# Five attention-weight transposes by DMA, with the tokens dealt otherwise to the logits' column groups, in a new order

## The chip, the cores and the metric

The kernel runs on one core of a Trainium2 chip. A core has a matrix engine (TensorE, PE in the profile, whose weight loads are listed as PEld), a vector engine (VectorE, DVE), a scalar engine (ScalarE, ACT), GpSimd (POOL) and SyncE (SP), which here issues nearly all DMAs. Each engine works through its own list of instructions in order, and they meet at semaphores. The metric is the device time of one execution in microseconds (us). Before the change it is 241.6 us, the median of 3 runs between 240.67 and 242.48.

## The reference

One transformer block over 2048 tokens of 512 features, in bfloat16, with adaptive layer norm. A conditioning vector gives six vectors of 512: shift, scale and gate for the attention half, and the same for the feed-forward half.

```python
mod = (_silu(c) @ w_mod).reshape(c.shape[0], 6, 1, -1)        # sa, ca, ga, sb, cb, gb
h = _layernorm(x, axis=-1) * (1 + ca) + sa
x = x + ga * _A_ref(h, A_wqkv, A_wo)
h = _layernorm(x, axis=-1) * (1 + cb) + sb
x = x + gb * _B_ref(h, B_w1, B_w3, B_w2)
```

`_A_ref` is local attention: 32 heads of 16 features; each token looks at itself and the 7 tokens 2, 4, ... 14 places back, positions before the start are masked, softmax over those 8, then the output projection `wo`. `_B_ref` is a gated feed-forward of width 1792: `silu(h @ w1) * (h @ w3) @ w2`.

## The kernel before, in words

The 2048 tokens are 16 tiles of 128, with tokens on the partitions (`x_sb`). Layer norm 1, its transposition (`ln_T`) and the projections q, k, v run on groups of 2, 2, 4, 4 and 4 tiles (`LN1`). q and k stay on the chip with features on the partitions; v goes to a scratch tensor in DRAM (`v_scratch_dram`) and comes back shifted.

Attention runs on pairs of tiles (`BLOCKS`: seven blocks, the last of two pairs).

- `logits`: for one tile, VectorE multiplies q with eight shifted views of k into `pq` (L742, 128 x 4096 elements). TensorE sums 16 features per head with an indicator matrix `E_sb` (L752): 16 matmuls of 32 output rows, in four column groups of the array that work side by side. Column group q gives 32 rows (the heads) of the logits for 32 tokens; a row holds 8 shifts by 32 tokens. Tile 0 starts with one more matmul (L749) that adds the mask `before`.
- `shift`, `exps`, `softmax` (L764, L769, L782, L794 to L797): maximum, subtraction, exponential, sum, reciprocal, product, on the PSUM bank of the pair; the weights `attn` are written to SBUF with the eight shifts of one token side by side.
- The weights are then turned, so that (token, shift) lies on the partitions and (token group, head) along the row: four TensorE transposes per pair (`turn`, L807) into a PSUM bank `ps_at`, and one ScalarE copy of 128 x 512 (L811) into `al`.
- `values`: four DMAs per tile (L820) gather v in the same arrangement into `vsh`; two buffers of their own and one, `vshx`, that lies where `wqkv` was. VectorE multiplies them with `al` (L827, 128 x 4096), TensorE sums over the shifts with `ind2` (L855, 32-column matmuls again), ScalarE copies (L861), a DMA transpose on SyncE's queue turns the result (`sb_ot<-sb_ac`), TensorE applies `wo` (L867), and VectorE adds it to `x_sb` with the row sum (L871).

Layer norm 2 takes that row sum: GpSimd gives the mean (L586), ScalarE the sum of squares (L590), GpSimd 1/sigma and the bias (L596, L597, L599), ScalarE the normalized tile (L601). Tiles are transposed on TensorE (L636) or by DMA (`sb_h<-sb_xn`, for groups 2 to 5) and modulated on ScalarE (L621 or L644). The feed-forward runs on groups of 2, 2, 4, 4, 2 and 2 tiles (`FFN`), 14 slices of 128 hidden features each: TensorE `w1` (L883), ScalarE Silu (L889), TensorE `w3` (L883 again), VectorE product (L892); then `w2` (L921, the last two tiles L909) and VectorE's residual addition (L931), and the store. At the start 24 matmuls on ones (L518) keep TensorE at work until the first data is there.

Nothing chooses the order of the work at run time. `_build` lists 1118 operations, each with its engine; `ORDER` is one written list of their numbers, from which every engine takes its own in that order, and `SLOTS` gives each pooled value its buffer or PSUM bank (8 banks). `synchronize` derives the waits. An operation waits for its producers and for the earlier users of its buffer; whatever stands behind it on its engine waits too. The `cost` and `dma` numbers in the calls are those of the planner that wrote the lists and have no effect in the kernel. All DMAs but one are issued by SyncE (`Program.dma`, L124).

## Time and profile before

| | before |
|---|---|
| median of 3 runs | 241.6 us (240.67 to 242.48) |
| the profiled execution | 241.33 us |
| its span | 239.6 us |
| TensorE busy | 231.9 us (97%) |
| VectorE busy | 179.2 us (75%) |
| ScalarE busy | 138.8 us (58%) |
| GpSimd busy | 30.0 us (13%) |
| L807 transposes | x32, 219 ns each, in 8 groups of four |
| L811 copies | x8, 598 ns each |
| DMA transposes | 20 of `sb_h<-sb_xn`, 16 of `sb_ot<-sb_ac` |
| moved by DMA | 38.85 MB |

The span is the time from the first to the last instruction in one profiled execution; the time of that execution is slightly longer. Busy times are unions of the instructions' records; matmuls overlap, so for TensorE the distance between starts says more than a record's length. In the lists, L12 is line 12 of the kernel, `x4` the number of instructions, and a bracket gives the idle time before an instruction and what ended it. SPq is SyncE issuing a DMA; the time from there to the landing is listed apart.

### The profile page before, as it was taken

The numbers are of one execution on the slowest core, as the hardware profiler recorded it, in microseconds if no ns is written. First come the engines' busy times: TensorE is split into PE (matmuls) and PEld (weight loads), VectorE is DVE, ScalarE is ACT, GpSimd is POOL, SyncE is SP. The second block draws the span as 40 slices with busy tenths as digits, with TensorE's granted clock in tenths as the row PEclk, the third lists the DMA queues.
The fourth block names the chain that finished last, engine by engine and source line by source line (L and its number), as shares of the span: only waits on it lengthen the run. The fifth ranks groups of instructions, "written<-read, shape, count | busy, mean of one in ns | idle before, by whom it ended". The sixth has DMA issues, their size and how long they took to land.

```text
span 239.6 us, 4572 instructions
## 1 busy us (share of the span) xinstructions
PE 231.9 (97%) x1806; PEld 135.9 (57%) x1806; DVE 179.2 (75%) x279; ACT 138.8 (58%) x267; POOL 30.0 (13%) x66
## 2 busy tenths in 40 slices
PE   7899999999999999999999999988999999999995
PEld 4676554545688684664444444433374484566774
DVE  5689999999999999999999989381555125234243
ACT  2289577899978737958735792636466043322210
POOL 4434000013002000420005220032020000000000
PEclk9999999999999999999999999999999999999999
DMA  6999999999999995998953995341300700010102
GB/s 210 373 336 309 138 244 299 214 270 310 335 291 255 250 204 168 248 191 240 228 153 90 198 228 58 96 122 36 77 22 12 100 0 0 3 43 2 47 22 66
DMA packets 46317, 38.85 MB, mean 162 GB/s; under 512 B 21704, under 2 KB 37080, under 8 KB 46296
## 3 DMA queue, kind: packets, MB, share of 16 engines
q1 hardware_dynamic: 46288, 38.56, 67.7%
q8 instruction: 14, 0.23, 0.4%
q14 instruction: 7, 0.06, 0.1%
q10 hardware_dynamic: 8, 0.00, 0.0%
HBM read 29.62 MB, written 4.21 MB: 141 GB/s over the span
## 4 chain that ended last, share of the span: by engine, by line
PE 79%; DMA 6%; DVE 5%; SPq 4%; ACT 2%; POOL 2%; issue 1%; DVEq 0%
PE pall L883 36%; PE pall L921 16%; PE pall L691 7%; PE pall L867 6%; DMA sb_x<-in_A_x_dram 5%; SPq L124 4%; PE pall L711 4%; PE pall L752 3%; PE pall L855 3%; PE pall L909 3%; DVE sb_pq L742 2%; DMA sb_ot<-sb_ac 1%; DVE sb_vsh L827 1%; POOL sb_nm L586 1%; DVE sb_st L555 1%
## 5 line engine op out<-in xcount | busy, mean ns | idle before, releaser
L883 PE MATMUL pall<-sb_h,sb_w 128*128 128x256 bf16 (+1 forms) x672 | 102.9, 308 | 1.7 <-ACT sb_sg L889 1.7
L883 PEld LDWEIGHTS pall<-sb_h,sb_w 128*128 128x128 bf16 x672 | 64.8, 98 | 38.1 <-ACT sb_sg L889 2.1
L892 DVE TENSOR_TENSOR sb_hh<-sb_sg,pall 128x256 bf16<-128x256 bf16 (+1 forms) x84 | 40.0, 506 | 37.8 <-PE pall L883 32.6
L889 ACT ACTIVATE sb_sg<-pall 128x256 bf16<-128x256 f32 (+1 forms) x84 | 35.7, 453 | 50.9 <-PE pall L883 49.0
L921 PE MATMUL pall<-sb_w,sb_hh 128*128 128x512 bf16 x196 | 45.1, 379 | 0.0
L742 DVE TENSOR_TENSOR sb_pq<-sb_q,sb_kT 128x4096 bf16<-128x4096 bf16 x16 | 36.4, 2283 | 0.0
L691 PE MATMUL pall<-sb_h,sb_wqkv 128*128 128x512 bf16 (+1 forms) x160 | 31.1, 336 | 0.4 <-DVE sb_st L555 0.4
L921 PEld LDWEIGHTS pall<-sb_w,sb_hh 128*128 128x128 bf16 x196 | 19.1, 98 | 21.2 <-issue 0.4
L827 DVE TENSOR_TENSOR sb_vsh<-sb_vsh,sb_al 128x4096 bf16<-128x4096 bf16 x12 | 27.3, 2285 | 0.0
L621 ACT ACTIVATE sb_h<-sb_h,sb_modc 128x512 bf16<-128x512 bf16 (+1 forms) x24 | 16.5, 742 | 9.5 <-DMA sb_h<-sb_xn 9.5
L691 PEld LDWEIGHTS pall<-sb_h,sb_wqkv 128*128 128x128 bf16 x160 | 14.6, 97 | 12.1 <-DVE sb_st L555 0.6
L931 DVE TENSOR_TENSOR sb_o<-pall,sb_x 128x512 bf16<-128x512 f32 (+1 forms) x18 | 11.1, 625 | 10.0 <-PE pall L921 6.2
L586 POOL TENSOR_SCALAR sb_nm<-sb_sx 128x2 f32<-128x2 f32 x8 | 3.7, 464 | 108.4 <-DVE sb_x L871 108.3
L867 PE MATMUL pall<-sb_wo,sb_ot 128*128 128x512 bf16 x64 | 15.8, 379 | 0.5 <-DMA sb_ot<-sb_ac 0.5
L711 PE MATMUL pall<-sb_wqkv,sb_h 128*128 128x512 bf16 x64 | 16.0, 379 | 0.0
L871 DVE SCALAR_TENSOR_TENSOR sb_x<-pall,sb_x 128x512 bf16<-128x512 f32 x16 | 10.9, 687 | 4.6 <-PE pall L867 4.2
L644 ACT ACTIVATE sb_h<-pall,sb_modc 128x256 bf16<-128x256 bf16 (+1 forms) x18 | 9.9, 611 | 7.5 <-DVE sb_modc L509 6.5
L590 ACT ACTIVATE sb_xn<-sb_x,sb_nm 128x512 bf16<-128x512 bf16 x16 | 11.4, 716 | 4.8 <-POOL sb_nm L586 4.8
L861 ACT ACTIVATE sb_ac<-pall 128x512 bf16<-128x512 f32 x16 | 9.4, 597 | 7.0 <-PE pall L855 6.8
L601 ACT ACTIVATE sb_xn<-sb_x,sb_nb,sb_rs 128x512 bf16<-128x512 bf16 x16 | 12.2, 804 | 1.5 <-POOL sb_nb L599 1.4
L555 DVE BATCH_NORM_STATS2 sb_st<-sb_x 128x6 f32<-128x512 bf16 x16 | 10.5, 680 | 1.4 <-DMA sb_x<-in_A_x_dram 1.4
L701 ACT ACTIVATE sb_kT<-pall 128x512 bf16<-128x512 f32 x16 | 9.6, 606 | 2.8 <-PE pall L691 2.7
(87 smaller groups left out, 206.7 us busy)
## 6 DMA issues: line engine op xcount, KB each, us to landing
sb_vsh<-v_scratch_dram SPq DMA_DIRECT2D x48, 256.0 KB, 5.4
sb_vshx<-v_scratch_dram SPq DMA_DIRECT2D x16, 256.0 KB, 5.1
sb_w<-in_B_w_dram SPq DMA_DIRECT2D x6, 512.0 KB, 7.2
sb_w<-in_B_w_dram SPq DMA_DIRECT2D x6, 384.0 KB, 4.1
v_scratch_dram<-sb_v SPq DMA_DIRECT2D x16, 128.0 KB, 6.0
out_dram<-sb_o SPq DMA_DIRECT2D x14, 128.0 KB, 1.8
sb_wqkv<-in_A_wqkv_dram SPq DMA_DIRECT2D x6, 256.0 KB, 6.5
sb_x<-in_A_x_dram SPq DMA_DIRECT2D x4, 256.0 KB, 6.5
```

What stands on the lines that cost most here:

```text
L555: o = p.op("dve", lambda e, T=T: e.bn_stats(st[:, T, :], x_sb[:, T, :]), 595, ("st", T), r=[vx[T]], w=[vs])
L601: p.op("act", lambda e, vn=vn, T=T: e.activation(vn.at[:], x_sb[:, T, :], ACT.Identity, bias=nb[:, T, :], scale=rs[:, NT + T, :]), c_act(5 ...
L621: return e.activation(vh.at[:, ft, 0:n * P], vh.at[:, ft, 0:n * P], ACT.Identity, bias=modc[:, 8 * which + ft:8 * which + ft + 1], scale=m ...
L691: ins = e.matmul(bank(vp)[:, j * n:(j + 1) * n], wqkv[:, t, col:col + P], vh.at[:, t, 0:n], start=(t == ORDER[0] and j == 0), stop=(t == O ...
L711: ins = e.matmul(bank(vp), vh.at[:, t, tt * P:(tt + 1) * P], wqkv[:, t, 2 * D:3 * D], start=(t == ORDER[0]), stop=(t == ORDER[-1]))
L742: return e.tensor_tensor(vp.at[:], in0, in1, ALU.mult)
L827: return e.tensor_tensor(v_w, v_w, a_w, ALU.mult)
L867: ins = e.matmul(bank(vy), vt.at[:, ft, :], wo[:, ft, :], start=(ft == 0), stop=(ft == KT - 1))
L883: ins = e.matmul(bank(vp)[:, 0:n], wt[:, t, fi * P:(fi + 1) * P], vh.at[:, t, 0:n], start=(t == 0), stop=(t == KT - 1))
L889: p.op("act", lambda e: e.activation(vt.at[:, 0:n], bank(vgp)[:, 0:n], ACT.Silu), c_act(n), k, r=[vgp], w=[vt], table="silu")
L892: p.op("dve", lambda e: e.tensor_tensor(vh_.at[:, 0:n], vt.at[:, 0:n], bank(vup)[:, 0:n], ALU.mult), c_dve(n), k, r=[vt, vup], w=[vh_])
L921: ins = e.matmul(bank(vz), vhh[fi].at[:, tt * P:(tt + 1) * P], w2[:, fi, :], start=(fi == 0), stop=(fi == NF - 1))
```

## The change

Before, column group q held the 32 tokens 32q to 32q + 31 of its tile, even ones first and odd ones behind. Now a column group holds one parity of two blocks of 32 tokens: group q takes the tokens 64a + 32 (q // 2) + q % 2 + 2b, for a in 0, 1 and b in 0 to 15. Each run of 16 tokens by 8 shifts of `attn` is then a plain block of 128 columns, and block after block the transposition gives `al` in the arrangement that L827 reads. That makes it one transposition of 128 x 512 in four square blocks, which a DMA can do.

- The mask for tile 0 has to reach two column groups, so L749 becomes two matmuls and the pattern of `before` changes.
- For the pairs that begin with tiles 0, 2 and 4 (`AT_PE`) TensorE and ScalarE do the turn as before. For the pairs 6, 8, 10, 12 and 14 the four transposes, the PSUM bank and the copy are replaced by one DMA transpose, issued by SyncE like all the others.
- `ORDER` and `SLOTS` are written anew, for 1113 operations and without five `ps_at` banks. The order differs on every engine. Two differences that the text below names: on SyncE the last load of x (tiles 12 to 15) comes ahead of the load of `wm_g[0]`, and on VectorE the residual additions of tiles 12 and 13, followed by one feed-forward product, come between the softmax of pair 14 and L827 of tiles 14 and 15.

```diff
     def dma(self, out, in_, key, packets, r=(), w=(), part=(), after=(), eng="sp", cost=450, group=None, transpose=False,
-            store=False, again=False, lat=None):
+            store=False, again=False, lat=None, hold=()):
...
+AT_PE = (0, 2, 4)
...
-    atb = [sb([P, 2, 32, W], bf, f"attn{i}") for i in range(NSM)]
-    alb = [sb([P, 2, 8, H], bf, f"al{i}") for i in range(3)]
+    atb = [sb([P, 2 * 32 * W], bf, f"attn{i}") for i in range(NSM)]
+    alb = [sb([P, 4, P], bf, f"al{i}") for i in range(3)]
...
-                                           pattern=[[-DIL, W], [1, 2], [2, 16]], channel_multiplier=0), 400, k, w=[vbefore])
+                                           pattern=[[-DIL, W], [64, 2], [2, 16]], channel_multiplier=0), 400, k, w=[vbefore])
...
                 if T == 0:
-                    e.matmul(PALL[0:32, c0:c0 + W * 32], ones[:, 0:32], before[:], start=True, stop=False, tile_position=(0, 0))
+                    for q in range(2):
+                        e.matmul(PALL[32 * q:32 * q + 32, c0:c0 + W * 32], ones[:, 0:32], before[:], start=True, stop=False, tile_position=(0, 32 * q))
                 for ft in range(KT):
                     for q in range(4):
-                        ins = e.matmul(PALL[32 * q:32 * q + 32, c0:c0 + W * 32], E_sb[:, ft, :], bass.AP(vp.at, ft * P + 32 * q, [[W * KT * P, P], [KT * P, W], [1, 2], [2, 16]]),
-                                       start=(ft == 0 and (T > 0 or q > 0)), stop=(ft == KT - 1), tile_position=(0, 32 * q))
+                        ins = e.matmul(PALL[32 * q:32 * q + 32, c0:c0 + W * 32], E_sb[:, ft, :], bass.AP(vp.at, ft * P + 32 * (q // 2) + q % 2, [[W * KT * P, P], [KT * P, W], [64, 2], [2, 16]]),
+                                       start=(ft == 0 and (T > 0 or q > 1)), stop=(ft == KT - 1), tile_position=(0, 32 * q))
...
-        vt, val = Val("ps_at", psum), Val("al", alpool)
+        val = Val("al", alpool)
+        if Ts[0] not in AT_PE:
+            p.dma(lambda: val.at[:], lambda: ve.at[0][:], ("at", Ts[0]), (128, 1024), r=[va], w=[val], hold=[ve], cost=1270, transpose=True)
+            return val
+        vt = Val("ps_at", psum)

         def turn(e):
             b = bank(vt).bitcast(bf)
-            for i in range(n):
-                at = b[:, i * 256:(i + 1) * 256].rearrange("p (q y h) -> p q y h", q=4, y=2)
-                for y in range(2):
-                    ins = e.transpose(at[:, :, y, :], bass.AP(ve.at[0], i * W * 32 + y * 16 * W, [[2 * W * 32, P], [1, P]]), ident[:])
+            for g in range(2 * n):
+                ins = e.transpose(b[:, g * P:(g + 1) * P], ve.at[0][:, g * P:(g + 1) * P], ident[:])
             return ins
...
 ORDER = [
...
 SLOTS = [
...
```

## The prediction

> **What bounds the kernel now.** I read the page first, then the busy times by stretch, the chain that ended last, and the timeline around the chain's only long gap.

> ```profile
> span 239.6 us, 4572 instructions
> PE 231.9 (97%) x1806; PEld 135.9 (57%) x1806; DVE 179.2 (75%) x279; ACT 138.8 (58%) x267; POOL 30.0 (13%) x66
> ...
> PE   7899999999999999999999999988999999999995
> ...
> DVE  5689999999999999999999989381555125234243
> ```

> TensorE is busy from end to end, VectorE nearly so until 150 us. The stretches (PE, PEld, DVE, ACT and POOL busy, clock, DMA share, GB/s) say it more sharply:

> ```profile
> 30.00:40.00 10.00, 10.00 (x79) 5.07 (x78) 9.94 (x12) 7.60 (x14) 0.55 (x1) 1.00 1.07 249
> ...
> 120.00:130.00 10.00, 10.00 (x87) 4.65 (x86) 10.00 (x11) 5.49 (x12) 2.07 (x2) 1.00 0.45 114
> ...
> 150.00:160.00 10.00, 10.00 (x57) 4.60 (x50) 5.61 (x10) 4.29 (x7) 2.08 (x1) 1.00 0.47 131
> 160.00:170.00 10.00, 8.10 (x48) 3.10 (x47) 4.00 (x5) 6.48 (x13) 1.55 (x4) 1.00 0.20 41
> ```

> The reader sees two engines full at once between 20 and 140 us, and one hole in TensorE at 160 to 170 us. The granted clock is 1.00 throughout, so TensorE's own steps can be added up. From one group's start to the next a feed-forward half (four matmuls, L883) takes 0.863 us at 512 columns and 0.437 at 256, seven matmuls of L921 1.51, four of L867, L711 or L691 0.863, a reduction (L752, L855) 0.44. Along the old order these steps make 231.4 us, from the first warm-up matmul at 1.24 us to the last; the trace ends them at 237.08. So 4.4 us are lost to waits: 0.9 before 58 us, 0.3 near 92, 3.05 between 155 and 174, 0.15 in small pieces. Behind the last matmul come 2.5 us of addition and store. The profiled execution took 241.33 us, 1.73 more than its span and 0.27 less than the median of the runs, 241.6. My sum is made against 241.33.

> **The change, part by part: the five transposes.** The chain shows what four transposes cost TensorE, and what a change between full-array and 32-column matmuls costs:

> ```profile
> 35.85 0.22 PE pall L807 x4
> ...
> 126.17 0.55 PE pall L855 x8
> 126.71 0.88 PE pall L752 x32
> 127.59 0.44 PE pall L855 x8
> 128.03 5.29 PE pall L883 x24
> ```

> Four transposes are one step of 0.22 us; five pairs give up 5 x 0.223 = 1.1 us, all of it on the full engine. Eight matmuls of L855 take 0.44 us behind other 32-column work and 0.55 behind L883; 24 matmuls of L883 take 5.29 behind L855 where 6 x 0.863 is 5.18. So each change of mode costs about 0.1 us. The old order of TensorE's work has 28 changes, the new one 32 (the reductions of tile pairs stand more often alone): 4 x 0.095 = +0.4 us. Tile 0's causal mask takes two small matmuls in place of one; they lie in different column groups and run together as the four groups of L752 do, under 0.1 us. Dealing the tokens otherwise keeps 16 matmuls of 256 columns per tile; only the middle step of the read pattern changes (64 tokens apart in place of 1), while the inner step stays 2 elements. Its price is not in the trace. Below, a cheaper read has nothing to give, since 16 x 256 / 4 columns already go in 0.44 us; above, four groups that no longer ran together would cost four times 0.44 on each of 16 tiles, +21 us. The inner step is the same, so I take 0. ScalarE loses five copies of L811 at 0.6 us; at 58% busy that alone is worth nothing. Sum so far: -1.1 + 0.4 = -0.7 us.

> **What the transposes become.** Each is now one DMA transpose of the shape of `sb_ot<-sb_ac`, whose view says:

> ```profile
> L124 SPq DMA_TRANSPOSE sb_ot<-sb_ac x16: 1189/1245/2137, 44.0 to 169.4; - x16
> ...
> DMA to landing us min/median/max: 2.3/2.8/6.6
> ```

> SyncE is held 1.25 us by each and waits at its head for the attention weights; the loads of L820 queued behind it wait too. From issue to landing it is 2.3 us in quiet stretches (from 128 us on) and 4 to 6.6 where the DMA share is about 1 (45 to 90 us). The attention multiply (L827) follows the weights in VectorE's order after 11.4 us of other work for tiles 6/7, 9.7 for 8/9, 4.6 for 10/11 and 1.8 for both 12/13 and 14/15 (rows of the old trace added up along the new order). The first two pairs cover any landing. For 10/11 a landing of 2.4 to 4 is covered. For 12/13 it isn't: 2.4 - 1.8 = 0.6 us of idle VectorE, of which TensorE has 0.7 us to spare before L855 needs the product. For 14/15 VectorE must wait some 4 us anyway, because two residual additions (L871) stand between, whose matmuls (L867) end near 156 us. I charge +0.4 us for this part, loads behind a waiting transpose included. [...] By the slow landing throughout, my charge would be 4.5 us instead of 0.4.

> **The hole at 160 us.**

> ```profile
> 157.75 2.29 DVE L827 TENSOR_TENSOR sb_vshx<-sb_vshx,sb_al 128x4096 bf16<-128x4096 bf16 x1
> 157.92 2.19 POOL L586 TENSOR_SCALAR sb_nm<-sb_sx 128x2 f32<-128x2 f32 x1 [16.87 <-DVE sb_x L871]
> ...
> 160.14 0.72 ACT L590 ACTIVATE sb_xn<-sb_x,sb_nm 128x512 bf16<-128x512 bf16 x1 [4.14 <-POOL sb_nm L586]
> ...
> 161.57 1.06 ACT L889 ACTIVATE sb_sg<-pall 128x512 bf16<-128x512 f32 x2
> ...
> 162.20 1.04 PE L883 MATMUL pall<-sb_h,sb_w 128*128 128x512 bf16 x4 [1.66 <-ACT sb_sg L889]
> ```

> A tiny GpSimd operation takes 2.19 us while L827 runs on VectorE (0.21 elsewhere), ScalarE stands 4.14 us before it in its queue, the Silu behind it frees its PSUM bank late, and TensorE stops. With the two short stops after it (0.6 and 0.7 us, the second before L867 at 171.8) this is the 3.05 us. In the new order a feed-forward multiply stands between the residual additions and L827, so GpSimd runs free; the Silus that TensorE needs next come before the normalization, and the ones behind it are needed 2 to 4 us later. What is late next: the variance step (L596) and L599 now fall beside L827, so the transposed tiles 12/13 land near 169 and their modulation (L621, four at 0.5 us steps) ends near 171.1, where TensorE wants them at 170.6. I keep 0.8 us of the 3.05: -2.25 us.

> **The front.** The new order issues the last x load ahead of a modulation load. The chain of before waits there (11.61 us of x load, then L555), and VectorE stood idle 0.45 us for it. TensorE reaches the second score reduction 0.8 us earlier than VectorE has the product ready; with the 0.45 back it waits +0.4 us. The remaining moves along both queues leave margins of a few tenths, which I count as nothing beyond the 0.4 above; without that cover they cost what rival 2 says.

> Sum: -0.7 + 0.4 - 2.25 + 0.4 = -2.15, and 241.33 - 2.15 = **239.2 us**, 1.0% under the median. About 1% is what a measurement of this kernel can tell from no change, so the forecast lies at that edge.

> **Rivals.** (1) All waits go: only the 0.7 and the whole 3.05 and half of the front's gain are won, nothing is charged, 237.3 us. For it: the freed slots on ScalarE. Against: L827 and L855 stand within tenths of each other in both orders. Chance 0.17. (2) The hole moves instead of going: the new end of attention has the same GpSimd steps beside L827 and 2.2 us stay, 241.4 us. For it: the same kind of wait occurs at 128 and 131 us before. Chance 0.24. (3) Slower: the transposes land late. It decides from a landing of 2.5 us for tiles 12/13 on (1.8 of work and 0.7 to spare). At 6.6 us, tiles 10/11 lose 2.0 less 1.6 to spare and 12/13 lose 4.8 less 0.7, and the loads behind a waiting transpose come 1 us later: 5.5 in place of 0.4, 244.3 us. Against: DMA is at 0.45 to 0.7 share in that stretch. Chance 0.13. (4) The dealing of tokens slows L752, or the new transposes are not of the form that I took: from 246 us, chance 0.03. The forecast itself (238.0 to 240.5) has 0.43.

> The forecast splits evenly at 1%, so faster is 0.17 + 0.22, slower is rival 3's larger part with rival 4 and some of rival 2's spread, 0.17, and 0.44 is left for within 1%. The range for 8 in 10 runs from rival 1 less 0.5 to just under rival 3: 236.8 to 243.8.

> **What would show it.** L807 at x12 and L811 at x3; five more DMA transposes into `sb_al`, landing in 2.3 to 3 us for the last two; L752 still 0.44 us a tile; TensorE without idle time above 0.8 us after 150 us; GpSimd's L586 near 157 us at 0.2 us. VectorE idle before L827 for `sb_al` by more than 1 us would mean rival 3, ScalarE idle for GpSimd again rival 2. The forecast is wrong if TensorE's waits before 150 us grow by over 1 us: I have only margins of tenths there.

## The result and the profile after

The changed kernel takes 249.31 us, the median of 6 runs between 248.78 and 249.76; the kernel before took 241.4 us beside it (6 runs, 240.67 to 242.95). The ratio is 1.0303, with a 95% interval of 1.0273 to 1.0333: 3% slower, where 239.2 us had been forecast, with 236.8 to 243.8 as the range. The profiled execution took 248.78 us. Its page (span, busy times, and the 40 slices of TensorE and of its granted clock):

```profile
span 247.0 us, 4522 instructions
...
PE 233.6 (95%) x1787; PEld 135.1 (55%) x1787; DVE 179.9 (73%) x279; ACT 137.2 (56%) x262; POOL 38.4 (16%) x66
...
PE   7899999999999499899899999989999999999995
...
PEclk9999999999999799999999999999999999999999
```

The single gap of before, at slices 27 and 28 (156 to 168 us), is shallower. A deeper one has opened in slice 14, at 80 us, and the clock dips with it. GpSimd (POOL) is busy for 38.4 us in place of 30.0, though it executes the same 66 instructions: the steps of layer norm 2 take 2.3 us more in sum, two of layer norm 1 (L564, L566) 6.1 us more. What the latter cost before 70 us, no run below tests. TensorE's waits, by what ended them (us in total, times, longest):

```profile
PE pall L637 <- ACT sb_xn L602: 3.7, 1, 3.7
PE pall L519 <- DVE sb_ones L376: 1.2, 1, 1.2
PE pall L859 <- DVE sb_vsh L831: 1.1, 1, 1.1
PE pall L505 <- DMA sb_wm_s<-in_w_mod_dram: 0.9, 1, 0.9
PE pall L871 <- DMA sb_ot<-sb_ac: 0.9, 1, 0.9
```

The lines have moved by 1 up to the logits' product, by 2 up to the softmax and by 4 behind it: L637 is the transposition of normalized tiles, L859 the sum over the shifts, L831 the value product, L597, L598 and L600 GpSimd's three steps of layer norm 2. The timeline around the 3.7 us (start, length, engine, instruction, and in brackets the idle time before it):

```profile
77.34 0.19 POOL L597 TENSOR_SCALAR sb_rs<-sb_var 128x2 f32<-128x2 f32 x1 [1.63 <-ACT sb_xn L591]
77.62 2.84 POOL L598 TENSOR_TENSOR sb_rs<-sb_rs,sb_cst 128x2 f32<-128x2 f32 x1
77.62 2.28 DVE L831 TENSOR_TENSOR sb_vsh<-sb_vsh,sb_al 128x4096 bf16<-128x4096 bf16 x1
...
80.48 2.29 DVE L743 TENSOR_TENSOR sb_pq<-sb_q,sb_kT 128x4096 bf16<-128x4096 bf16 x1
80.54 2.28 POOL L600 TENSOR_TENSOR sb_nb<-sb_nm,sb_rs 128x2 f32<-128x2 f32 x1
82.85 1.52 ACT L602 ACTIVATE sb_xn<-sb_x,sb_nb,sb_rs 128x512 bf16<-128x512 bf16 x2 [4.30 <-POOL sb_nb L600]
83.72 0.39 PE L637 MATMUL pall<-sb_ident,sb_xn 128*128 128x128 bf16 x2 [3.66 <-ACT sb_xn L602]
```

Read it from the bottom. TensorE waits for the normalized tiles 2 and 3, ScalarE for their bias, and GpSimd needs 5.5 us for three operations on 128 x 2 numbers. The power (L598) starts in the same moment as a large VectorE product and takes 2.84 us; the product of two columns (L600) starts 0.06 us after the next large one, takes 2.28 us and ends 0.05 us behind it. VectorE's products keep their 2.28 us. In the kernel before, the same steps stood ahead of the value product:

```profile
75.78 2.12 DVE L892 TENSOR_TENSOR sb_hh<-sb_sg,pall 128x256 bf16<-128x256 bf16 x6
76.07 0.19 POOL L596 TENSOR_SCALAR sb_rs<-sb_var 128x2 f32<-128x2 f32 x1 [1.64 <-ACT sb_xn L590]
76.35 0.70 POOL L597 TENSOR_TENSOR sb_rs<-sb_rs,sb_cst 128x2 f32<-128x2 f32 x1
77.12 0.19 POOL L599 TENSOR_TENSOR sb_nb<-sb_nm,sb_rs 128x2 f32<-128x2 f32 x1
...
77.82 2.29 DVE L827 TENSOR_TENSOR sb_vsh<-sb_vsh,sb_al 128x4096 bf16<-128x4096 bf16 x1
```

Six small feed-forward products cover GpSimd there, and L827 begins 0.5 us after it is done. The new order puts two small products (0.79 us) in that place.

The gap costs more than its length. TensorE's clock by stretches of 2 us (PE, PEld, DVE, ACT, POOL busy, clock, DMA share, GB/s):

```profile
80.00:82.00 2.00, 0.06 (x1) 0.00 (x0) 2.00 (x3) 0.00 (x0) 1.92 (x2) 1.00 1.05 245
82.00:84.00 2.00, 0.28 (x2) 0.13 (x2) 0.77 (x1) 1.15 (x2) 0.82 (x1) 0.82 1.09 289
84.00:86.00 2.00, 2.00 (x18) 1.06 (x17) 0.00 (x0) 0.97 (x3) 0.00 (x0) 0.50 1.16 201
86.00:88.00 2.00, 2.00 (x11) 0.94 (x8) 1.27 (x2) 2.00 (x5) 0.00 (x0) 0.82 0.80 218
88.00:90.00 2.00, 2.00 (x41) 1.44 (x40) 1.35 (x1) 0.17 (x2) 0.00 (x0) 1.00 0.78 239
```

TensorE is back at work from 84 us on, but at half its clock, then at 0.82: 2 x 0.50 + 2 x 0.18 = 1.4 us more. Together about 5 of the 7.4 us by which the span grew.

For the whole span I took the distance from each matmul's start to the next one's, subtracted 0.213 us per 512 columns (a quarter of that for 32-column work), and summed what is left by stage. The 0.213 is an allowance of mine, just under what the traces show: seven matmuls of 512 columns take 1.51 us, 0.216 each, and the 16 of 256 columns in a 32-column reduction 0.44 us, a quarter of that per column. This "excess" holds waits, low clock and changes of mode alike; the stages go by each run's own time. In us:

| stage | before | after |
|---|---|---|
| 0 to 22 us | 5.5 | 6.6 |
| 22 to 70 | 3.4 | 4.0 |
| 70 to 90 | 0.9 | 6.3 |
| 90 to 125 | 1.3 | 4.3 |
| 125 to 150 | 1.0 | 0.9 |
| 150 to 180 | 3.6 | 1.9 |
| behind 180 | 0.9 | 1.1 |
| sum | 16.7 | 25.1 |
| span less sum (the work) | 222.9 | 221.9 |

So the work shrank by 1.0 us (this follows from the count of matmuls at the lengths subtracted), the stage of the old hole by 1.7, and 10 us came in elsewhere, 8.4 of them between 70 and 125 us.

### The profile page after: what moved, and what is told of

Read it like the earlier page. It is cut to its first block, busy times and chain, and to the rows that moved or that the text cites. A ratio compares the mean times of both kernels' runs of the same rounds, so it can differ in the third digit from the quotient of the medians.

```text
span 247.0 us, 4522 instructions
## 1 busy us (share of the span) xinstructions
PE 233.6 (95%) x1787; PEld 135.1 (55%) x1787; DVE 179.9 (73%) x279; ACT 137.2 (56%) x262; POOL 38.4 (16%) x66
## 4 chain that ended last, share of the span: by engine, by line
PE 69%; DMA 10%; DVE 7%; POOL 5%; ACT 4%; SPq 3%; issue 2%; DVEq 0%
PE pall L887 34%; PE pall L925 10%; PE pall L692 8%; PE pall L871 4%; PE pall L712 4%; DMA sb_x<-in_A_x_dram 3%; SPq L124 3%; PE pall L859 3%; POOL sb_nb L600 3%; PE pall L913 2%; PE pall L754 2%; DMA sb_ot<-sb_ac 2%; DMA v_scratch_dram<-sb_v 2%; POOL sb_rs L598 2%; DMA sb_al<-sb_attn 2%
## 5 line engine op out<-in xcount | busy, mean ns | idle before, releaser
L896 DVE TENSOR_TENSOR sb_hh<-sb_sg,pall 128x256 bf16<-128x256 bf16 (+1 forms) x84 | 40.6, 506 | 38.3 <-PE pall L887 36.3
L893 ACT ACTIVATE sb_sg<-pall 128x256 bf16<-128x256 f32 (+1 forms) x84 | 36.4, 454 | 51.3 <-PE pall L887 46.6
L831 DVE TENSOR_TENSOR sb_vsh<-sb_vsh,sb_al 128x4096 bf16<-128x4096 bf16 x12 | 27.4, 2285 | 1.7 <-DMA sb_al<-sb_attn 1.7
L587 POOL TENSOR_SCALAR sb_nm<-sb_sx 128x2 f32<-128x2 f32 x8 | 1.7, 218 | 126.9 <-DVE sb_x L875 126.9
L871 PE MATMUL pall<-sb_wo,sb_ot 128*128 128x512 bf16 x64 | 15.8, 379 | 1.1 <-DMA sb_ot<-sb_ac 0.9
L591 ACT ACTIVATE sb_xn<-sb_x,sb_nm 128x512 bf16<-128x512 bf16 x16 | 11.4, 714 | 6.6 <-POOL sb_nm L587 6.5
L701 ACT ACTIVATE sb_q<-pall 128x512 bf16<-128x512 f32 x16 | 9.1, 602 | 3.5 <-PE pall L692 3.5
```

What stands on the lines that cost most here:

```text
L591: p.op("act", lambda e, vn=vn, T=T: e.activation(vn.at[:], x_sb[:, T, :], ACT.Square, bias=nm[:, T, :], accum_out=var[:, T, :]), c_act(512 ...
L831: return e.tensor_tensor(v_w, v_w, a_w, ALU.mult)
L871: ins = e.matmul(bank(vy), vt.at[:, ft, :], wo[:, ft, :], start=(ft == 0), stop=(ft == KT - 1))
L893: p.op("act", lambda e: e.activation(vt.at[:, 0:n], bank(vgp)[:, 0:n], ACT.Silu), c_act(n), k, r=[vgp], w=[vt], table="silu")
L896: p.op("dve", lambda e: e.tensor_tensor(vh_.at[:, 0:n], vt.at[:, 0:n], bank(vup)[:, 0:n], ALU.mult), c_dve(n), k, r=[vt, vup], w=[vh_])
```

## The experiments

Three suspects: the **order**, by putting GpSimd's small steps beside VectorE's large products; the **transposes**, by landing late or by holding SyncE's queue; the **dealing** of tokens. All ratios below are against the kernel before, run beside them, with 95% intervals.

### The dealing alone

All eight pairs turn on TensorE again, in the old order.

```diff
-AT_PE = (0, 2, 4)
+AT_PE = (0, 2, 4, 6, 8, 10, 12, 14)
...
 ORDER = [
...
```

> The new dealing of tokens alone: the matmuls of L752 read with the other stride and fill the other column groups, all eight pairs are still turned on TensorE and copied by ScalarE, and the order and the buffers are those of the kernel before. If the dealing costs nothing (theory of the order, theory of the late transposes): 241.4 us, within 1%. If the dealing is the cause (64-token stride slower to read, or the half-added mask): up to 249.

Measured: 1.0012 (0.9978 to 1.0046). The dealing is free within that interval, as forecast.

### The five transposes in the old order

The new dealing and the five DMA transposes, each right behind its softmax product in the list; everything else keeps the old order and the old buffers.

```diff
 ORDER = [
...
```

> Dealing and the five DMA transposes, in the order of the kernel before: each transpose is issued right behind its softmax product, and nothing else moves. Theory of the order (GpSimd's small steps of the second layer norm fall beside VectorE's large products only in the new order): 240 to 242 us, no 3.8 us hole near 80 us, the hole at 160 us as before. Theory of the late transposes (3.5 to 8.5 us to land, and SyncE's queue held for it): 244 to 249, with VectorE waiting for sb_al before its value products.

Measured: 1.075 (1.0651 to 1.0849), the slowest kernel of all; both expectations missed. There is no GpSimd stretch near 77 us, but there are other gaps, two of them large. The first, on SyncE's queue (SPq) and TensorE:

```profile
75.01 1.19 SPq L124 DMA_TRANSPOSE sb_al<-sb_attn  x1
76.24 0.58 SPq L124 DMA_DIRECT2D sb_w<-in_B_w_dram  x1
...
80.33 3.41 PE L887 MATMUL pall<-sb_h,sb_w 128*128 128x256 bf16 x16 [4.51 <-DMA sb_w<-in_B_w_dram]
```

A weight load stood behind the transpose, which waited for the softmax until 75.0 us; TensorE waited 4.51 us for the weights. Later the gathers of v come late in the same way: VectorE waits up to 7.3 us for them, and TensorE 7.0 at 158 us. The transposes themselves landed sooner here than in the changed kernel, in 2.4 us at the median.

### The same, further back in SyncE's queue

Again the old order, but each transpose behind the transfers that SyncE issued ahead of the softmax product's end in the trace of before. Only the places of five operations differ from the last kernel.

```diff
 ORDER = [
...
```

> Dealing and five DMA transposes in the order of the kernel before, as in the run of 261.6 us, but each transpose stands in SyncE's queue behind the transfers that the kernel before issues ahead of the softmax product's end. Theory of the queue (SyncE issues in order, and a transpose that waits for the softmax holds the loads of weights and values behind it): 241 to 243.5 us. If the transposes cost by themselves, wherever they stand: 250 or more.

Measured: 1.0176 (1.0101 to 1.0252), 246.15 us. Of the 7.5% nearly 6 go by moving five entries in one queue, so the place in the queue was most of the cost. The time is still above what I expected: VectorE waits 4.7 us for gathers of v. I read this as the five issues of 1.2 us pushing them back, which no run shows by itself. Nor is it shown that these transposes need a new order: the changed kernel (1.0303) is slower than this one, and with its gap closed (1.0111 below) the intervals overlap.

### The new order without DMA transposes

Turns and copies of all pairs are back on TensorE and ScalarE, inserted where the trace of the changed kernel has room.

```diff
-AT_PE = (0, 2, 4)
+AT_PE = (0, 2, 4, 6, 8, 10, 12, 14)
...
 ORDER = [
...
```

> The new order, but the attention weights of the last five pairs are turned on TensorE and copied by ScalarE again; the turns and copies stand in the places that the trace of the changed kernel leaves for them. Theory of the order: 247 to 250 us, with the hole near 80 us still there. Theory of the late transposes: 239 to 242.

Measured: 1.0082 (1.0052 to 1.0112), 245.01 us, between the two expectations. Taken by the time alone this puts most of the loss on the transposes. The trace says otherwise:

```profile
77.77 2.85 POOL L598 TENSOR_TENSOR sb_rs<-sb_rs,sb_cst 128x2 f32<-128x2 f32 x1
...
80.70 0.20 POOL L600 TENSOR_TENSOR sb_nb<-sb_nm,sb_rs 128x2 f32<-128x2 f32 x1
...
81.55 2.28 DVE L743 TENSOR_TENSOR sb_pq<-sb_q,sb_kT 128x4096 bf16<-128x4096 bf16 x1
```

The power is stretched just as before, but the logits' product comes 0.85 us after L600 instead of 0.06 us ahead of it, because a small product of VectorE ahead of it waited 0.83 us for TensorE. L600 takes 0.20 us, TensorE loses 0.8 us at 81 us instead of 3.8, and its clock stays at 1.00. This run undid the gap by accident, so it can't separate the two causes; the next ones do.

### GpSimd's three steps away from the product

First by giving the steps of tiles 2 and 3 to VectorE. This kernel leaves out the power for these two tiles; a plain product stands in its place.

```diff
+LN2_DVE = (2,)
...
+        eng = "dve" if i in LN2_DVE else "pool"
-        o = p.op("pool", lambda e: e.tensor_scalar(rsn, var[:, i:i + n, 0], ...
+        o = p.op(eng, lambda e: e.tensor_scalar(rsn, var[:, i:i + n, 0], ...
...
+        o = p.op(eng, (lambda e: e.tensor_tensor(rsn, rsn, rsn, ALU.mult)) if eng == "dve" else
...
 ORDER = [
...
```

> The changed kernel, but the three small steps of the second layer norm of tiles 2 and 3 (scale, power, product; L597 to L600) run on VectorE right before the value product that GpSimd had them beside. [...] Theory of the order, with GpSimd beside VectorE as its mechanism: the 3.8 us hole near 80 us and the low clock behind it go, 244 to 245.5 us. If GpSimd's long steps there are not what holds TensorE: 248.5 to 249.5, with the hole left.

Measured: 1.0063 (1.0025 to 1.0101), 244.06 us, as the first theory expected. The five transposes are in this kernel as in the changed one, and its clock is 1.00 from 78 to 86 us.

Then by one added wait, with nothing else changed; operation 437 is the value product of tile 5, 682 is L600:

```diff
+HOLD = ((437, 682),)
...
+        for a, b in HOLD:
+            p.ops[a].deps[p.ops[b]] = True
         p.place(ORDER, SLOTS)
```

> The changed kernel with one wait more: VectorE's value product of pair 4 (L831, 77.6 us) starts only when GpSimd's three small steps of tiles 2 and 3 (L597 to L600) are done. Theory that GpSimd cannot run beside such a product and loses the race by 0.1 us: VectorE starts about 1 us later, the three steps take 1.2 us instead of 5.4, the hole near 80 us goes, 244 to 245.5 us, as where these steps were on VectorE. If GpSimd's length is not what holds TensorE, the added wait can only cost: 249 to 251.

Measured: 1.0111 (1.0052 to 1.017), 244.7 us. A kernel that waits more is 1.9% of before faster than the changed one, 4.6 us. In its trace (lines moved by 3):

```profile
77.59 0.70 POOL L601 TENSOR_TENSOR sb_rs<-sb_rs,sb_cst 128x2 f32<-128x2 f32 x1
...
78.36 0.19 POOL L603 TENSOR_TENSOR sb_nb<-sb_nm,sb_rs 128x2 f32<-128x2 f32 x1
78.59 2.29 DVE L834 TENSOR_TENSOR sb_vsh<-sb_vsh,sb_al 128x4096 bf16<-128x4096 bf16 x1 [0.92 <-POOL sb_nb L603]
```

VectorE gives 0.92 us and GpSimd's steps are done at 78.55 instead of 82.82. The excess from 70 to 90 us falls from 6.3 to 2.1 us, and the clock is 1.00 throughout. With this the main cause is shown.

### The other stretched steps

```diff
-HOLD = ((437, 682),)
+HOLD = ((437, 682), (507, 770), (530, 858))
...
 ORDER = [
...
```

> As the run before, and the same wait at the two other places where the trace shows GpSimd's step stretched beside a large product: the logits' product at 108.7 us waits for the steps of tiles 4 to 7, the value product at 134.9 us for those of tiles 8 and 9. If each stretched step costs as the first does, the waits of TensorE at 109 and 115 us (0.74 and 1.06 us) go: 242 to 244. If VectorE is what bounds there, its 1.6 and 1.2 us of waiting eat the gain: within 0.5 us of the run with one wait.

Measured: 1.0165 (1.011 to 1.0221), 246.09 us: not better than one wait, and above both expectations. The steps of tiles 4 to 7 no longer stretch, but VectorE's waits for them (1.8 and 1.1 us, besides the 0.9) come out as waits of TensorE for its products: the excess from 125 to 150 us goes from 0.9 to 2.2, that from 90 to 125 only from 4.0 to 3.7. Waiting pays where VectorE has time to spare, and here it had none. The same places without a wait, by moving the steps of tiles 2 to 7 to VectorE (the power is left out for these six tiles):

```diff
-LN2_DVE = (2,)
+LN2_DVE = (2, 4, 6)
...
 ORDER = [
...
```

> The changed kernel with the three small steps of tiles 2 to 7 (not only 2 and 3) on VectorE, right before its next large product; a plain product stands for the power, so these six tiles are scaled wrongly. If GpSimd beside the logits' products at 108.7 and 111.9 us makes the two losses of 0.74 and 1.06 us on TensorE at 110 and 116 us: 242 to 243 us, about 1.5 us under the run with tiles 2 and 3 alone (1.0063 of before). If the new order's later transposes and products make them: no difference, 243.5 to 244.5.

Measured: 1.0034 (0.9998 to 1.0069), 243.32 us, beside 1.0063 with tiles 2 and 3 alone. The ratios differ by 0.7 us in the direction expected, but their intervals overlap and the time lies between the two expectations. What the later stretches cost is not settled.

### The transposes' own price, with the gap closed

With the added wait in both, the last two pairs (12 and 14), then all five, go back to TensorE and ScalarE.

```diff
-AT_PE = (0, 2, 4)
+AT_PE = (0, 2, 4, 12, 14)
...
 ORDER = [
...
 SLOTS = [
...
```

> The changed kernel with the wait at 77.6 us, and the weights of pairs 12 and 14 turned on TensorE and copied by ScalarE again (DMA transposes only for pairs 6, 8 and 10). If the late landing of these two is what is left (VectorE waits 1.9 and 1.5 us for sb_al, TensorE 1.28 us behind the first): 242.8 to 243.8 us, about 1 us under the run with the wait alone (1.011 of before). If VectorE's order holds TensorE there anyway: no difference, 244 to 245.

Measured: 1.0101 (1.0059 to 1.0143), against 1.0111: no difference in the time. The wait of TensorE behind `sb_al` goes as expected (excess from 150 to 180 us 1.2 instead of 2.2), but in the profiled execution the start lost 0.9 us more, half of it in TensorE's wait for the modulation's weights, a stage that this edit leaves as it was.

```diff
-AT_PE = (0, 2, 4, 12, 14)
+AT_PE = (0, 2, 4, 6, 8, 10, 12, 14)
...
 ORDER = [
...
 SLOTS = [
...
```

> The new order with the wait at 77.6 us and no DMA transpose of weights at all (all eight pairs turned on TensorE). What is then left above the kernel before is the new order's own: if the DMA transposes cost anything net beside the stretched steps, this is under the run with five of them (1.011 of before), 1.000 to 1.006, 242 to 243.4 us; if the order alone makes it, 1.009 to 1.013, 244.1 to 245.

Measured: 1.007 (1.0042 to 1.0097), 243.99 us, between the two expectations. TensorE is then full where the old hole was:

```profile
150.00:160.00 10.00, 10.00 (x59) 4.34 (x58) 8.04 (x8) 5.04 (x9) 0.00 (x0) 1.00 0.28 66
160.00:170.00 10.00, 10.00 (x51) 4.62 (x50) 6.96 (x8) 4.66 (x10) 4.40 (x4) 1.00 0.51 146
```

By the rows, five DMA transposes save 1.1 us of TensorE's steps, and the kernel is no faster with them than without (1.0111 against 1.007; the intervals overlap). In the traces they lose it again at 160 us: the excess from 150 to 180 us is 2.2 with them and 0.8 without. And the new order, with the gap closed and no DMA transpose of weights, is still 0.7% slower than the old one: against before its excess is 1.5 us more up to 70 us, 1.2 from 70 to 90 and 2.5 from 90 to 125, and 2.8 less from 150 to 180.

### The old hole, in the kernel before

The reading that the forecast was built on, tried by itself. In the kernel before, the value product of tile 15 waits for GpSimd's L586, that of tile 14 for the three steps behind it.

```diff
+HOLD = ((596, 954), (586, 959))
```

> The kernel before the change, with two such waits in pair 14: L827 of tile 15 waits for GpSimd's L586 (2.19 us beside it in the trace of before, 0.22 alone), L827 of tile 14 for the three steps behind it. The reading of the prediction, that the hole of 1.82 us at 160 us comes from GpSimd beside L827: the hole goes and 0.5 us more behind it, 239 to 240.5 us against 242.4. If the hole is only VectorE's order, the 1.7 us that VectorE starts later come on top: 242.5 to 244.

Measured: 0.9934 (0.9896 to 0.9972), 240.62 us. The same kernel in five rounds:

> The kernel before with the two waits of pair 14 again, in five rounds, since three left a ratio between 0.9896 and 0.9972. If the gain is that of the hole (1.82 us at 160 us, of which 0.88 comes back at 164 us): a ratio of 0.993 to 0.997. If it was chance: an interval that holds 1.

Measured: 0.9911 (0.988 to 0.9943), 240.99 us beside 242.75, somewhat more than expected. The trace of the first three rounds (lines moved by 3):

```profile
158.79 0.22 POOL L589 TENSOR_SCALAR sb_nm<-sb_sx 128x2 f32<-128x2 f32 x1 [16.88 <-DVE sb_x L874]
...
159.04 2.29 DVE L830 TENSOR_TENSOR sb_vshx<-sb_vshx,sb_al 128x4096 bf16<-128x4096 bf16 x1 [0.34 <-POOL sb_nm L589]
...
162.25 0.19 POOL L602 TENSOR_TENSOR sb_nb<-sb_nm,sb_rs 128x2 f32<-128x2 f32 x1
...
162.55 2.29 DVE L830 TENSOR_TENSOR sb_vsh<-sb_vsh,sb_al 128x4096 bf16<-128x4096 bf16 x1 [1.21 <-POOL sb_nb L602]
```

L586 takes 0.22 us instead of 2.19, VectorE gives 0.34 and 1.21 us where it has time, and the stop of TensorE at 160 us is gone; at 164 us 0.9 us of excess is left. From 150 to 180 us the excess falls by 1.4 us. This version beats both kernels, with the old turns on TensorE.

## Why the prediction was wrong

**The step that failed** is the last of the sum: "The remaining moves along both queues leave margins of a few tenths, which I count as nothing". I added up durations from rows of the old trace along the new order. For GpSimd's steps that does not work: 0.20 or 0.70 us is their length beside small products, and 2.0 to 2.8 us beside a large one, so here a margin of a tenth decided over 2 us each time (0.70 us became 2.84, and 0.20 became 2.28). The changed kernel lost it twice in a row, at 77.6 and at 80.5 us, and the low clock came on top: 5 us in place of nothing. The added wait gave 4.6 of them back. From 90 to 125 us 3.0 more were lost, of which the new order without DMA transposes keeps 2.5; what makes them stays open.

**The rival with the right mechanism** was the second, GpSimd beside the value product. I looked for it only where the old hole was and let it cost the 2.2 us of that hole, 241.4 us. It came 80 us earlier and with a price that I had not in the sum, the clock. "TensorE's waits before 150 us grow by over 1 us" is the sign that I had named, and it is what happened.

**The old hole**: forecast -2.25 us for it and up to +0.4 for late transposes, -1.85 in that stage. The stage from 150 to 180 us gave -1.7, and without DMA transposes -2.8. The reading of it was right, and the two waits in the kernel before confirm it from the other side: the stop goes when GpSimd's steps are let through.

**The transposes on TensorE**: -1.1 us was forecast. The 1.0 us less of work in the changed trace is 19 matmuls fewer at a fixed length each, so it repeats that sum and doesn't test it. The changes of mode are 32 in place of 28, as forecast; their +0.4 is part of the excess and can't be told apart there. The dealing costs nothing that the run could tell, as taken.

**The late transposes**, a term of the sum that was mis-sized. I took 2.4 us for the landing of 12/13, from the quiet rows of `sb_ot` (the loaded ones there are 3.4 to 6.6 us, not 4 to 6.6 as I wrote); it was 4:

```profile
152.83 1.20 SPq L124 DMA_TRANSPOSE sb_al<-sb_attn  x1
...
156.82 2.29 DVE L831 TENSOR_TENSOR sb_vshx<-sb_vshx,sb_al 128x4096 bf16<-128x4096 bf16 x1 [1.83 <-DMA sb_al<-sb_attn]
...
161.37 0.62 PE L859 MATMUL pall<-sb_vsh,sb_ind 128*32 128x512 bf16 x8 [1.06 <-DVE sb_vsh L831]
```

VectorE waits 1.83 us and TensorE 1.06, where +0.4 stood in the sum. By the sign that I had named (over 1 us of VectorE's idle time) this is the third rival's mechanism, at a fifth of its price (1.06 of 5.5 us): 6/7, 8/9 and 10/11 were covered, as reckoned, also against a landing of 8.5 us. The product of 14/15 waits 1.72 us for its transpose too, with no wait of TensorE behind it. In all seven traces that have it, the transpose of 12/13 lands after 3.8 to 4.4 us, in the old order as well; that of 14/15 takes 2.3 and 2.4 us in the two old-order runs and 3.8 to 4.5 in the new order. Why, no run settles.

**The front**: +0.4 us forecast, +1.1 measured in the changed trace; TensorE waits 0.9 us for the modulation's weights (`sb_wm_s`). SyncE issues that load at 1.31 us in both kernels, so my reason (the last load of x) is not what ended this wait; why it ends later isn't settled.

## What to carry to other kernels

When an order is written anew, check by name every small operation that changes its length by what runs beside it, here GpSimd's beside VectorE's large products (0.20 us against 2.28), along the whole span and not only around the gap that one wants to close. Where such a race was close, the wait that let the small operations go first cost VectorE 0.92 us and gave back 4.6 us of the time (77.6 us); two more waits, of 1.8 and 1.1 us, where VectorE had no time to spare, gained nothing (1.0165 against 1.0111). A transfer that must wait for data belongs in its queue behind those that need not: five transposes at the wrong place in SyncE's queue cost 7.5%, and at a better one 1.8%.

## What the runs showed of the hardware

```profile
164.00:166.00 2.00, 0.73 (x2) 0.28 (x3) 2.00 (x3) 0.81 (x1) 0.00 (x0) 0.50 0.00 0
166.00:168.00 2.00, 2.00 (x6) 0.60 (x4) 1.97 (x3) 0.00 (x0) 0.00 (x0) 0.50 0.00 0
168.00:170.00 2.00, 2.00 (x20) 0.56 (x19) 1.20 (x2) 0.54 (x2) 0.00 (x0) 0.68 0.08 19
```

  After the stop of 1.66 us in the kernel before (162.20 us), the clock is 1.00, and so it is after one of 2.2 us at 91 us in the old-order run with the transposes further back. But the low clock came after shorter stops too: in the old-order run two stops of 0.64 and 1.14 us, at 119 and 120 us, are followed by clocks of 0.87, 0.50 and 0.77 in the rows of 2 us from 120 to 126. What sets this case apart from the stop of 2.2 us, no run settles.
- A DMA transpose of 128 x 512 between two buffers on the chip (`sb_al<-sb_attn`) lands 2.3 to 11.7 us after its issue in these runs (the extremes are in the two old-order ones), and holds SyncE 1.2 to 1.3 us.
